# A two-branch conformer layer, forward and backward: four more normalised tiles and three copies out of PSUM on ScalarE instead of VectorE, in a new order of instructions

## The chip, the cores and the metric

The kernel runs on one core of one Trainium2 chip. The metric is the device time of one execution in microseconds (us). Five engines work side by side, each through its own queue of instructions in order: PE (TensorE, matmuls), DVE (VectorE), ACT (ScalarE), POOL (GpSimd) and SP (SyncE, here only the issuer of DMA transfers). They wait for each other through semaphores.

## The reference

A layer with two branches is computed for x of shape 2 x 4000 x 144 (bf16), and then its vector-Jacobian product for a given grad_out: the output and the gradients of x and of the seven weights. Cut to what matters:

```python
xa = _layernorm(x)                                   # (x - mean) / sqrt(var + eps)
q, k, v = split(xa @ w_qkv)
p = softmax(q @ k.T * D ** (-0.5))                   # 4000 x 4000 for each batch
glob = (p @ v) @ w_att_out
u, g = split(gelu(xa @ w_mlp_in))
loc = (u * dwconv(_layernorm(g), dw_csgu)) @ w_mlp_out
m = concat(glob, loc)
out = x + (m + dwconv(m, dw_merge)) @ w_merge        # 5 taps each
out, vjp = jax.vjp(layer, x, *weights); grads = vjp(grad_out)
```

## The kernel before

A batch's 4000 tokens are 32 tiles of 125 tokens (PB = 125); D = 144 is split into 128 and 16 rows wherever it is the contraction dimension. The attention of both batches is one loop over 64 tiles of queries. For each tile, `quad` (L1184) multiplies the queries with all keys, a chunk of 1000 keys at a time into a PSUM tile `ps`: 128 rows from `xaT_m` (L1187) and then the 16 remainder rows (L1194). `S_min` (L1209) moves the scores to `Pbuf` on DVE with a running minimum; after four chunks L1211 makes one number of the minima, and `P_exp` (L1215) does the Exp on ACT, in place. SP transposes the result by DMA to `PT` (L1219). Further on come dP (L1225 on ACT, L1226 on DVE, or L1223 on DVE alone) into `Sbuf`, its transposed form `ST` (L1405), the products `yz` with PT (L1236) and ST (L1266) and the gradient sums `X` (L1322, gathered in `acc` by L1327 and L1329). The work of the other branch and of the merge convolution is laid between the tiles; L590, L596, L621, L640 and L644 are its elementwise steps on DVE. The second batch is loaded and prepared while the first is still worked on: `gq` is its grad_out, `xa_aug` its x.

The head, up to the first Exp, concerns the first batch alone and works on four groups g of eight tiles. `ln_st` (L362) takes statistics on DVE, `ln_mv` (L368 to L373) makes the variance on DVE, and POOL raises it to the power −1/2 (L374); `ln_nm` (L378) makes minus mean over deviation, and `ln` normalises the eight tiles j of the group into `xa_aug`: on ACT where j is a multiple of four (L383, 8 tiles of 32), on DVE where it is odd (L385, 16), on POOL for the rest (L387, 8). Then `xat` transposes the group on PE: the main 128 rows into one PSUM tile, which ACT copies to `xaT_m` (L392, L393), and 112 rows into another, of which the last 16 are copied to `R` (L396, and L397 on DVE, 16 partitions x 1000 elements). From R, SP copies them to four partition groups `XR` (L399), out of which later tiles take the remainder rows; the first tile takes them out of R itself. `jit_q` and the following lines make a tile's queries (L1346 to L1349 `qb`, L1354 transposes, L1355 `qt`). At the same time the head fuses weights (L170 to L219: `two`, `Q`, `RW`, `cols`) and scales the merge weights tap by tap (`sWm`, L238 on ACT, L240 on POOL). `dwt` is the small DMA of the merge convolution's weights (L157), which PE needs at L215. 36 filler matmuls (`warm`, L192) lie between PE's first instructions.

No engine chooses what comes next. The class `Planner` holds a table `ORDER` with a list of numbers for each engine: the program's instructions (for PE, runs of them) are numbered as they are written, and the list says in which sequence they stand; each is chained to the one ahead of it on its engine. The lists have 1385 entries for PE, 2521 for DVE, 1642 for ACT, 423 for POOL and 826 for SP. They were written down as literal numbers, so every edit that adds or removes an instruction renumbers them.

Of the kernel before, what the change touches and what calls it, by code (L numbers as in the profile page):

```python
# [337 lines left out]
def pre_pieces(k, W, b, S, pst):  # L338
# [4 lines left out]
    if True:  # L343
# [36 lines left out]
        def ln(g):  # L380
            for j in range(8 * g, 8 * g + 8):
                if S.act_ln and j % 4 == 0:
                    nc.scalar.activation(S.xa_aug[:, j, 0:D], x_tp[:, j, :], ACT.Identity, scale=S.rstd_x[:, j:j + 1], bias=nmr[:, j:j + 1])  # L383
                elif j % 2:
                    nc.vector.tensor_scalar(S.xa_aug[:, j, 0:D], x_tp[:, j, :], S.rstd_x[:, j:j + 1], nmr[:, j:j + 1], op0=ALU.mult, op1=ALU.add)  # L385
                else:
                    nc.gpsimd.tensor_scalar(S.xa_aug[:, j, 0:D], x_tp[:, j, :], S.rstd_x[:, j:j + 1], nmr[:, j:j + 1], op0=ALU.mult, op1=ALU.add)  # L387

        def xat(g):
# [7 lines left out]
            nc.vector.tensor_copy(v8(S.R, 8 * g, 8)[96:112], pr[96:112, :, 0:PB])  # L397
# [378 lines left out]
class Planner:  # L776

    ORDER = {
# [1414 lines left out]
```

## Time and profile before

| | us |
|---|---|
| median of three runs | 1150.79 (1150.02 to 1152.15) |
| the profiled execution | 1152.39 |
| its span, from the first to the last instruction in the profile | 1150.5 |
| PE busy | 1118.8 |
| DVE busy | 1021.0 |
| ACT busy | 906.5 |
| POOL busy | 249.5 |

The profile is of one execution. A row of the timeline has its start (us from the span's beginning), its length, the engine, the line of the kernel, the operation, its output and input tiles with their sizes, how many instructions like it follow each other (xN, the length then is that of all of them), and in square brackets the idle time ahead of it with what ended that. PEld are PE's weight loads, and SPq and ACTq the issues of DMAs by these engines: their length is the issue's, not the transfer's. A row of the table by stage has the stage, its length, the busy time of PE, PEld, DVE, ACT and POOL (with the number of instructions), the granted clock of TensorE, the share of time in which the DMA engines were busy, and GB/s. A row of the waits says which engine at which line waited for what: us in total, how often, and the longest. Instructions of one engine overlap slightly, so the sum of their lengths can exceed the time between two starts.

### The profile page before, as it was taken

What the parts mean: (1) busy time and instruction counts of PE and PEld (TensorE: products, weight loads), DVE (VectorE), ACT (ScalarE), POOL (GpSimd) and SP (SyncE); (2) the same over time, 40 slices, a digit from 0 to 9 for tenths busy, and PEclk for the clock granted to TensorE, in tenths of its full rate; (3) what the DMA queues carried; (4) which work ended last, traced back from release to release, by engine and by line L of the source; (5) the groups of instructions that cost most, each with busy time, mean ns of one, the idle gap of its engine ahead of it and who ended that gap; (6) DMA issues with size and microseconds to landing.
All of it is one profiled execution on the core that took longest, in us unless ns stands there. A gap on an engine that the chain in (4) does not pass through costs nothing.

```text
span 1150.5 us, 35851 instructions
## 1 busy us (share of the span) xinstructions
PE 1118.8 (97%) x14293; PEld 868.7 (76%) x14293; DVE 1021.0 (89%) x3063; ACT 906.5 (79%) x1641; POOL 249.5 (22%) x427
## 2 busy tenths in 40 slices
PE   6999999999999999999999999999999999999998
PEld 3667777777777677777777777777777777699987
DVE  8699999999999998877999999999999997667656
ACT  5999898899898767777989889888889877615372
POOL 8111112111121113431001111111111112013642
PEclk9999999999999999999999999999999999999999
DMA  4688887979988989998988989888888899978973
GB/s 117 155 160 176 173 181 158 192 159 173 174 166 159 188 181 182 201 187 183 207 183 178 171 158 168 161 181 152 173 174 154 187 177 183 224 173 219 245 144 101
DMA packets 680887, 200.72 MB, mean 174 GB/s; under 512 B 657815, under 2 KB 674093, under 8 KB 680699
## 3 DMA queue, kind: packets, MB, share of 16 engines
q1 hardware_dynamic: 678352, 194.69, 84.6%
q0 software_dynamic: 2192, 3.62, 1.1%
q8 instruction: 111, 1.82, 0.7%
q14 instruction: 56, 0.46, 0.1%
q10 hardware_dynamic: 176, 0.12, 0.0%
HBM read 24.62 MB, written 18.01 MB: 37 GB/s over the span
## 4 chain that ended last, share of the span: by engine, by line
PE 64%; DMA 13%; DVE 11%; ACT 7%; issue 2%; SPq 1%; POOL 1%; ACTq 0%; DVEq 0%; POOLq 0%
PE X L1322 18%; PE ps L1187 14%; PE yz L1236 8%; PE yz L1266 8%; PE ps L1194 5%; DMA PT<-Pbuf 5%; DVE Pbuf L1209 4%; ACT Pbuf L1215 3%; PE po L1708 2%; DMA ST<-Sbuf 2%; PE pd L610 1%; DVE Sbuf L1226 1%; PE pj L1147 1%; ACT Sbuf L1225 1%; DMA go_h<-in_grad_out_dram 1%
## 5 line engine op out<-in xcount | busy, mean ns | idle before, releaser
L1209 DVE TENSOR_SCALAR_CACHE_REDUCE Pbuf<-ps 125x1000 bf16<-125x1000 f32 x256 | 306.2, 1197 | 30.1 <-PE ps L1194 22.4
L1225 ACT CAST Sbuf<-ps 125x1000 bf16<-125x1000 f32 x249 | 248.7, 999 | 86.7 <-PE ps L1194 66.2
L1215 ACT ACTIVATE Pbuf<-Pbuf,nm 125x1000 bf16<-125x1000 bf16 x256 | 284.9, 1144 | 4.4 <-DVE nm L1211 4.2
L1322 PE MATMUL X<-QBs,Pbuf 125*128 125x144 bf16 x2048 | 281.1, 226 | 0.2 <-POOL QBs L1256 0.2
L1322 PE MATMUL X<-QBs,Sbuf 125*128 125x144 bf16 x2048 | 281.3, 226 | 0.0
L1187 PE MATMUL ps<-xaT_m,qt 128*128 128x500 bf16 x1024 | 260.6, 374 | 5.0 <-DVE Pbuf L1209 3.5
L1322 PEld LDWEIGHTS <-Sbuf 125*128 125x128 bf16 x2048 | 198.2, 98 | 18.8 <-issue 18.5
L1322 PEld LDWEIGHTS <-Pbuf 125*128 125x128 bf16 x2048 | 200.2, 98 | 1.3 <-issue 1.1
L1226 DVE TENSOR_TENSOR Sbuf<-Sbuf,Pbuf 125x1024 bf16<-125x1024 bf16 x249 | 170.8, 690 | 7.9 <-ACT Sbuf L1225 6.0
L1236 PE MATMUL yz<-xa_aug,PT 125*128 125x145 bf16 x2048 | 151.0, 227 | 6.5 <-DMA PT<-Pbuf 6.4
L1266 PE MATMUL yz<-xa_aug,ST 125*128 125x144 bf16 x2048 | 150.8, 228 | 3.6 <-DMA ST<-Sbuf 2.4
L1236 PEld LDWEIGHTS <-PT 125*128 125x128 bf16 x2048 | 130.7, 98 | 21.6 <-DMA PT<-Pbuf 10.5
L1187 PEld LDWEIGHTS <-qt 128*128 128x128 bf16 x1024 | 91.4, 97 | 68.6 <-issue 7.0
L1266 PEld LDWEIGHTS <-ST 125*128 125x128 bf16 x2048 | 132.9, 98 | 12.2 <-issue 7.1
L1329 DVE TENSOR_TENSOR acc<-X,acc 125x432 f32<-125x432 f32 (+1 forms) x204 | 109.8, 548 | 15.3 <-PE X L1322 14.8
L1256 POOL TENSOR_TENSOR QBs<-g,g 125x144 bf16<-125x144 f32 x64 | 35.2, 550 | 379.2 <-ACT g L1255 290.9
L1194 PEld LDWEIGHTS <-qt 16*128 16x128 bf16 x1024 | 26.3, 91 | 108.9 <-issue 108.9
L1194 PE MATMUL ps<-XR,qt 16*128 16x500 bf16 x1016 | 100.4, 380 | 0.0
L681 POOL TENSOR_SCALAR l_w<-ring,nc,c 125x144 f32<-125x144 bf16 x64 | 31.8, 504 | 167.0 <-DVE nc L677 122.4
L653 DVE TENSOR_TENSOR l_prod<-ring,Wc 125x720 bf16<-125x720 bf16 x128 | 65.9, 535 | 0.2
L1611 PE MATMUL Hps<-Yg,go_h 125*128 125x144 bf16 x640 | 54.3, 226 | 0.0
L600 POOL TENSOR_TENSOR rsr<-ve,mhalf 125x2 f32<-125x2 f32 x32 | 25.4, 795 | 126.9 <-DVE ve L599 107.4
(540 smaller groups left out, 1946.4 us busy)
## 6 DMA issues: line engine op xcount, KB each, us to landing
Yn_d<-yn SPq DMA_DIRECT2D x64, 36.0 KB
Zn_d<-qb SPq DMA_DIRECT2D x64, 36.0 KB
ug_d<-ugr SPq DMA_DIRECT2D x32, 72.0 KB
Yg<-Yn_d SPq DMA_DIRECT2D x8, 288.0 KB
Yg<-ug_d SPq DMA_DIRECT2D x8, 288.0 KB
Zn<-Zn_d SPq DMA_DIRECT2D x4, 576.0 KB
PT<-Pbuf SPq DMA_TRANSPOSE x128
ST<-Sbuf SPq DMA_TRANSPOSE x128
```

Source lines behind the costliest of these rows:

```text
L653: nc.vector.tensor_tensor(prod[:, bi].rearrange("p a b -> p (a b)"), ring[:, a, p + bi:p + bi + 5, :].rearrange("p a b -> p (a b)"), W.Wc[ ...
L1187: mm = nc.tensor.matmul(pp[r // 2][:, r % 2, 0:CH], QT[i][:, 2 * h, :], bs(i)[0].xaT_m[:, c * CH:(c + 1) * CH], start=True, stop=False)
L1194: nc.tensor.matmul(pp[r // 2][:, r % 2, 0:CH], QT[i][rs, 2 * h + 1, :], xr, start=False, stop=True)
L1209: nc.vector.tensor_scalar(pv(pc(i, c2)), src, -1.0, 3.0e38, op0=ALU.mult, op1=ALU.min, accum_out=NM[i][:, c2:c2 + 1])
L1215: nc.scalar.activation(v, v, ACT.Exp, bias=NM[i][:, 4:5], scale=-1.0)
L1225: nc.scalar.copy(pv(sc(i, c2)), src)
L1226: nc.vector.tensor_tensor(sc(i, c2), sc(i, c2), pc(i, c2), op=ALU.mult)
L1236: nc.tensor.matmul(Yw, PT[0:PB, pos(i, j), :], S.xa_aug[:, j, 0:D + 1], start=(j == 0), stop=(j == NB - 1))
L1266: nc.tensor.matmul(Zw, ST[0:PB, j, :], S.xa_aug[:, j, 0:D], start=(j == 0), stop=(j == NB - 1))
L1322: nc.tensor.matmul(X[:, jj, :], l, r, start=(n_ == 0), stop=(n_ == len(ops) - 1))
L1329: nc.vector.tensor_tensor(av, X[0:PB, 0:nj, :], av, op=ALU.add)
L1611: nc.tensor.matmul(H[0:rows, a // 3, (a % 3) * D:(a % 3 + 1) * D], lhs, self.src[b][h][:, 2 + j, :], start=(n == 0 and a % 3 == 0), stop=( ...
```

## The change

Two lines of `pre_pieces` change. In `ln`, the tiles j = 3, 11, 19 and 27 of the first batch pass from DVE to ACT: ACT has 12, DVE 12, POOL 8 of the 32. In `xat`, the copy of the remainder rows to R passes from DVE to ACT for the groups 1, 2 and 3; group 0 keeps it on DVE.

```diff
-                if S.act_ln and j % 4 == 0:
+                if S.act_ln and j % 8 in (0, 3, 4):
...
-            nc.vector.tensor_copy(v8(S.R, 8 * g, 8)[96:112], pr[96:112, :, 0:PB])
+            (nc.scalar.copy if g else nc.vector.tensor_copy)(v8(S.R, 8 * g, 8)[96:112], pr[96:112, :, 0:PB])
...
     ORDER = {
-        "PE": [36, 37, 38, 39, 40, 41, 0, 1, 42, 2, 3, 4, 5, 43, 6, 7, 8, 44, 9, 10, 11, 53, 12, 45, 13, 46, 14, 47, 15, 16, 17, 48, 18, 54, 19, 49,
+        "PE": [36, 37, 38, 39, 40, 41, 0, 42, 1, 2, 3, 4, 43, 5, 6, 7, 44, 8, 9, 10, 53, 45, 11, 46, 12, 47, 13, 14, 15, 54, 16, 17, 18, 48, 19, 20,
```

All five lists of `ORDER` are replaced. DVE's now has 2514 entries and ACT's 1649, the others as many as before. On PE 542 of the 1385 runs stand at another place, by half a place on average and by ten at most; on POOL and SP single rows move by up to 54 and 68 places. The last 989 rows of PE, and what the other engines do beside them, are in the same order. In the head, dwt is now SP's fourth DMA (before its fourteenth), the 128-row part of w_qkv is issued on ACT ahead of the 16-row part, and PE multiplies chunk 1 of the first tile ahead of the transposes (L1354) of the next tile's queries. These are the places of which the prediction speaks.

ACT in the head, from its first weights to the first copy of transposed x. Before:

```order
L205 ACTIVATE RW<-hps 16x144
L205 ACTIVATE Q_283<-hps 128x144
L383 ACTIVATE xa_aug_114<-Sbuf,lnnm_101,rstd_x_65 125x144 x2
L217 CAST cols<-hps 128x2x5
L393 COPY xaT_m_118<-pt 128x1000
L238 ACTIVATE sWm_309<-raw,cols 128x144 x2
```

And of the change:

```order
L205 ACTIVATE Q_283<-hps 128x144
L217 CAST cols<-hps 128x2x5
L238 ACTIVATE sWm_309<-raw,cols 128x144
L205 ACTIVATE RW<-hps 16x144
L238 ACTIVATE sWm_309<-raw,cols 128x144
L218 CAST cols<-hps 16x2x5
L238 ACTIVATE sWm_309<-raw,cols 128x144
L219 ACTIVATE cols<-cols 128x4
L238 ACTIVATE sWm_309<-raw,cols 128x144
L383 ACTIVATE xa_aug_114<-Sbuf,lnnm_101,rstd_x_65 125x144 x3
L238 ACTIVATE sWm_309<-raw,cols 128x144 x2
L393 COPY xaT_m_118<-pt 128x1000
```

Four taps (sWm) and the casts for them have moved ahead of the normalised tiles of group 0, of which ACT now has three.

POOL in the head, from the power of group 2 to the tiles j18 and j22. Before:

```order
L374 TENSOR_TENSOR rstd_x_65<-lnve_100,mhalf 125x8
L2024 MEMSET A_dwc 128x240
L387 TENSOR_SCALAR xa_aug_114<-Sbuf,rstd_x_65,lnnm_101 125x144 x2
L374 TENSOR_TENSOR rstd_x_65<-lnve_100,mhalf 125x8
L65 MEMSET go_q_95 29x288
```

And of the change:

```order
L374 TENSOR_TENSOR rstd_x_65<-lnve_100,mhalf 125x8
L1119 MEMSET Pbuf 125x144x3
L240 TENSOR_SCALAR sWm_310<-raw,cols 128x144
L374 TENSOR_TENSOR rstd_x_65<-lnve_100,mhalf 125x8
L387 TENSOR_SCALAR xa_aug_114<-Sbuf,rstd_x_65,lnnm_101 125x144 x3
```

The two tiles of group 2 now stand behind the power of group 3, and a memset and a tap stand ahead of that.

SP while the second batch is loaded, from one store of Zn to the pair of PT transposes some 450 us into the kernel. Before:

```order
L1271 DMA Zn_d_71<-qb_128 128x144
L1405 DMA_TRANSPOSE ST<-Sbuf 128x16x128
L43 DMA xa_aug_8229<-in_x_dram 13x8x144
L1248 DMA Yn_d_69<-yn_132 128x144
L43 DMA gq<-in_grad_out_dram 13x576
L1405 DMA_TRANSPOSE ST<-Sbuf 128x16x128
L1219 DMA_TRANSPOSE PT<-Pbuf 128x16x128 x2
```

And of the change:

```order
L1405 DMA_TRANSPOSE ST<-Sbuf 128x16x128
L42 DMA gq<-in_grad_out_dram 112x576
L1271 DMA Zn_d_71<-qb_128 128x144
L42 DMA gq<-in_grad_out_dram 112x576 x2
L43 DMA gq<-in_grad_out_dram 13x576 x2
L1405 DMA_TRANSPOSE ST<-Sbuf 128x16x128
L43 DMA gq<-in_grad_out_dram 13x576
L1219 DMA_TRANSPOSE PT<-Pbuf 128x16x128 x2
```

Loads of gq and the store of Zn have moved between the first ST transpose and the PT pair. On DVE, some 74 us into the kernel, L621 stands two L1209 earlier than it did; before, it was two instructions ahead of the L1209 of which the prediction speaks.

More of the change, by code (lines that the diff above doesn't have):

```diff
@@ L778 @@
     ORDER = {
[51 rows of a table removed]
[51 rows of a table added]
             1347, 1342, 1348, 1337, 1343, 1324, 1353, 1344, 1345, 1349, 1346, 1352, 1325, 1350, 1361, 1363, 1362, 1365, 1364, 1354, 1355, 1369, 1371,
             1370, 1356, 1372, 1373, 1357, 1375, 1358, 1367, 1376, 1377, 1374, 1379, 1378, 1380, 1359, 1360, 1381, 1383, 1382, 1384, 1366, 1368],
-        "DVE": [0, 2, 1, 3, 4, 10, 5, 11, 9, 8, 6, 7, 12, 14, 15, 13, 16, 17, 40, 43, 25, 18, 44, 20, 22, 23, 19, 32, 24, 21, 34, 33, 35, 36, 26, 28,
[102 rows of a table removed]
-        "Activation": [1, 0, 4, 5, 2, 3, 7, 6, 8, 9, 10, 13, 29, 32, 14, 15, 11, 33, 16, 17, 18, 12, 37, 35, 34, 19, 20, 21, 24, 22, 23, 31, 27, 26,
[64 rows of a table removed]
-        "Pool": [8, 5, 15, 4, 11, 0, 12, 10, 1, 3, 47, 7, 2, 16, 18, 6, 19, 17, 41, 25, 26, 24, 50, 33, 32, 31, 9, 53, 37, 38, 20, 30, 42, 23, 13,
[43 rows of a table removed]
+        "DVE": [2, 1, 0, 3, 4, 5, 11, 10, 8, 6, 9, 7, 12, 14, 15, 16, 17, 13, 20, 25, 22, 23, 18, 24, 21, 19, 32, 41, 37, 28, 26, 33, 34, 35, 42, 29,
[102 rows of a table added]
+        "Activation": [0, 1, 2, 4, 3, 5, 6, 11, 36, 7, 40, 12, 45, 13, 42, 9, 8, 10, 39, 43, 14, 41, 15, 16, 19, 17, 18, 20, 37, 38, 21, 22, 23, 26,
[64 rows of a table added]
+        "Pool": [4, 10, 0, 50, 1, 6, 2, 7, 13, 8, 15, 9, 11, 16, 18, 19, 5, 17, 25, 26, 24, 41, 20, 31, 32, 33, 37, 47, 38, 14, 35, 22, 28, 30, 21,
[43 rows of a table added]
             805, 788, 813, 761, 821, 771, 789, 798, 804, 820, 797, 807, 822, 823, 814, 808, 806, 824, 825, 815],
```

518 rows, old and new, of the table ORDER are left out of this document.

## The prediction

> **What bounds the kernel now.** I read the page first (busy shares, slices), then a table by stage, then TensorE's waits, then the head instruction by instruction.
>
> ```profile
> PE 1118.8 (97%) x14293; PEld 868.7 (76%) x14293; DVE 1021.0 (89%) x3063; ACT 906.5 (79%) x1641; POOL 249.5 (22%) x427
> PE   6999999999999999999999999999999999999998
> ```
>
> TensorE is busy for 97% of the span, and its only poor slice is the first. The same by stage (columns: busy us of PE, PE's weight loads, DVE, ACT, POOL, then the granted clock):
>
> ```profile
> 0.00:28.60 28.60, 18.79 (x147) 11.43 (x147) 23.85 (x93) 15.60 (x45) 23.31 (x49) 1.00 0.45 117
> 28.60:100.00 71.40, 68.69 (x781) 49.31 (x780) 58.13 (x138) 68.08 (x138) 9.11 (x19) 1.00 0.76 164
> 520.00:1120.00 600.00, 591.11 (x7769) 471.14 (x7767) 522.47 (x1553) 461.58 (x817) 118.25 (x195) 1.00 0.90 182
> ```
>
> PE is idle for 9.8 us of the first 28.6 (28.60 − 18.79), for 2.7 of the next 71, and then for 1.5% (8.9 of 600). So the change, whose named edits all lie in the first 28 us, can only act there; behind it, a new order can only reshuffle the small waits. These are PE's three largest waits in the head, and then the largest of the rest of the kernel:
>
> ```profile
> PE hps L170 <- DMA raw<-in_w_qkv_dram: 6.3, 1, 6.3
> PE hps L215 <- DMA dwt<-in_dw_merge_dram: 1.4, 1, 1.4
> PE pt L1354 <- DVE R L397: 1.4, 1, 1.4
> ...
> PE yz L1236 <- DMA PT<-Pbuf: 6.4, 11, 1.0
> PE ps L1187 <- DVE Pbuf L1209: 3.5, 12, 0.9
> PE yz L1266 <- DMA ST<-Sbuf: 2.4, 3, 1.2
> ```
>
> Two head waits are named by the change's own parts: 1.4 us on the R copy of DVE, and 1.4 us on the DMA of dwt, which now is issued fourth instead of fourteenth. Much of PE's "busy" time in the head is filler, so what counts there is the chain to the first Exp; from then on PE is 96% busy (68.69 of 71.40), and what the first Exp gains or loses I pass on to the end one for one.
>
> **The change, part by part.** The chain's last links before, from PE, ACT and DVE:
>
> ```profile
> 21.78 0.60 PE L392 MATMUL pt<-ident,xa_aug 125*128 125x125 bf16 x8
> 23.36 0.72 ACT L238 ACTIVATE sWm<-raw,cols 128x144 bf16<-128x144 bf16 x2
> 23.98 0.98 ACT L393 COPY xaT_m<-pt 128x1000 bf16<-128x1000 bf16 x1
> 24.93 0.69 DVE L397 COPY R<-pt 16x1000 bf16<-16x1000 bf16 x1
> 26.50 0.59 PE L1194 MATMUL ps<-R,qt 16*128 16x500 bf16 x2
> 27.12 1.20 DVE L1209 TENSOR_SCALAR_CACHE_REDUCE Pbuf<-ps 125x1000 bf16<-125x1000 f32 x1 [0.19 <-PE ps L1194]
> 28.56 2.15 ACT L1215 ACTIVATE Pbuf<-Pbuf,nm 125x1000 bf16<-125x1000 bf16 x2
> ```
>
> *DVE loses* four tiles and three R copies. Four tiles take 1.00 us (row below), so 0.25 each and 1.0 in all; three copies at 0.69 are 2.07. Together 3.1 us less on an engine that was busy 16.34 of the 18.89 us of the stretch in which the chain runs:
>
> ```profile
> 21.26 1.00 DVE L385 TENSOR_SCALAR xa_aug<-Sbuf,rstd_x,lnnm 125x144 bf16<-125x144 bf16 x4
> 9.67:28.56 18.89, 16.60 (x135) 10.27 (x135) 16.34 (x63) 13.02 (x38) 15.82 (x31) 1.00 0.37 90
> 9.67 0.89 ACT L383 ACTIVATE xa_aug<-Sbuf,lnnm,rstd_x 125x144 bf16<-125x144 bf16 x2
> ```
>
> *ACT gains* them. A pair of its tiles takes 0.89, so four take 1.8. The trace has no 16x1000 copy on ACT. Bounds: 0.69 (DVE's row for the same copy) and 0.98 (ACT's copy of 128x1000, the same number of elements per partition). I take 0.98, the nearest row for engine and length: 2.9 for three. ACT gets 4.7 us into 18.89 − 13.02 = 5.9 us of idle time. It fits, but with 1.2 us to spare. [...]
>
> *What it does to the chain.* Let T be the time at which chunk 2's main transposes end, before 22.4 (21.78 + 0.60). ACT now runs four copies in a row from T: xaT of chunk 2, R, xaT of chunk 3, R. ACT's instructions overlap a little (the taps of 23.36 last 0.72, and the copy begins 0.62 behind them): 0.88 apart, the last R copy ends at T + 3 x 0.88 + 0.98 = T + 3.6; before, it ended on DVE at 25.62 = T + 3.2. Behind it now follow only the remainder matmuls, 0.59, and the 1.44 from L1209 to Exp (27.12 to 28.56): Exp at T + 5.7, against T + 6.2. So the new tail of the head is 0.45 **shorter** for equal T, although the copy itself is later.
>
> T is where the orders differ. Chunk 2's tiles j18 and j22 are POOL's:
>
> ```profile
> 13.31 0.69 DVE L397 COPY R<-pt 16x1000 bf16<-16x1000 bf16 x1 [1.20 <-PE pt L396]
> 15.59 0.30 DVE L373 TENSOR_SCALAR lnve<-lnve 125x8 f32<-125x8 f32 x1
> 13.37 0.74 POOL L1119 MEMSET Pbuf<- 125x432 bf16 x1
> 18.13 0.90 POOL L387 TENSOR_SCALAR xa_aug<-Sbuf,rstd_x,lnnm 125x144 bf16<-125x144 bf16 x2 [0.27 <-DVE lnnm L378]
> 19.00 1.64 POOL L374 TENSOR_TENSOR rstd_x<-lnve,mhalf 125x8 f32<-125x8 f32 x1
> ```
>
> POOL now does the power of group 2, the memset (0.74), a tap (0.37, near ACT's pair at 0.72), the power of group 3 (1.64) and only then j18 and j22 (0.9). Group 2's variance (L373) comes behind the first R copy on DVE, as before, with seven statistics instead of five ahead of it (about +0.6): 16.4 if that copy ends at 14.0 again. Then 16.4 + 1.64 + 0.74 + 0.37 + 1.64 + 0.9 = 21.7, the transposes of these last two tiles, T = 22.1: first Exp at 27.8, **0.75 early**. But the first R copy itself may move, for chunk 0's transposes do:
>
> ```profile
> 1.49 0.39 ACTq L154 DMA_DIRECT2D raw<-in_w_qkv_dram  x1
> 10.99 1.02 PE L392 MATMUL pt<-ident,xa_aug 125*128 125x125 bf16 x8
> ```
>
> In ACT's new order four taps and three small casts (4 x 0.36 plus, an estimate from the overlap, about 0.35: 1.8) stand between Q and its tiles, which began at 9.67 before. They now begin at 11.5, and three of them last till 12.8; the transposes, which ended at 12.0, end some 1.1 later. Against that, PE no longer waits for dwt, and the large part of w_qkv goes first on ACT's queue, one issue (0.4) earlier. I take +0.7 for the copy, which about cancels the 0.75. **Head: 0**, between −1.2 (the copy 0.4 early, nothing lost) and +0.7 (1.1 late, with some tenths of ACT's new load on the path).
>
> *The rest of the order.* One place gains plainly:
>
> ```profile
> 74.32 0.30 DVE L621 TENSOR_TENSOR ring<-dugr,hgr 125x288 bf16<-125x288 bf16 x1
> 74.54 0.45 DVE L644 TENSOR_TENSOR gpr<-l_sq,l_q 125x576 bf16<-125x576 bf16 x1
> 76.16 1.01 PE L1187 MATMUL ps<-xaT_m,qt 128*128 128x500 bf16 x4 [0.60 <-DVE Pbuf L1209]
> ```
>
> PE's 0.60 wait is for the L1209 that follows these two, and L621 (0.22 from start to start) has moved ahead of earlier work of DVE's, which in this stage is idle for 13 us (71.40 − 58.13): **−0.2**; 0, if it had no idle time just there. One place loses, SP between 452 and 463:
>
> ```profile
> 452.20 1.60 SPq L1405 DMA_TRANSPOSE ST<-Sbuf  x1
> 453.84 0.55 SPq L43 DMA_DIRECT2D xa_aug<-in_x_dram  x1
> 454.49 0.35 SPq L1248 DMA_DIRECT2D Yn_d<-yn  x1
> 454.89 0.69 SPq L43 DMA_DIRECT2D gq<-in_grad_out_dram  x1
> 455.76 3.12 SPq L1405 DMA_TRANSPOSE ST<-Sbuf  x1
> 458.98 3.78 SPq L1219 DMA_TRANSPOSE PT<-Pbuf  x2
> 463.52 0.56 PEld L1236 LDWEIGHTS <-PT 125*128 125x128 bf16 x9 [0.22 <-issue]
> ```
>
> From the first ST transpose to the PT pair three small transfers are issued, and PE takes up PT 0.8 us after the pair's issue. Now seven are, at about 0.45 each: PT is 1.8 later. PE's order moves the first L1236 only behind four more transposes (0.2 to 0.4). I take **+0.2**, since SP waits here for its data and part of the seven may fall into that; bounds 0 and +1.4. The other waits (some 16 us in the three rows above and smaller ones) I leave as they are, plus or minus 3: POOL's and SP's runs move by a handful of places everywhere with no one direction.
>
> *Sum.* 0 − 0.2 + 0.2 = 0 on the profiled execution's 1152.39 (span 1150.5 and 1.9 around it). That execution lies 1.6 above the median of the runs shown, 1150.79, so the forecast on the median is **1150.8**.
>
> **The rivals.**
> - *The head keeps what it was given.* If w_qkv lands early enough that ACT's taps are through before group 0's statistics, both PE waits of 1.4 fall away and nothing replaces them: −2.8, with −0.2 above 1147.8. For it: both waits are in the rows, and DVE's relief is real. Against: POOL's two powers before j18.
> - *SP becomes late where x and grad_out of the second batch are loaded.* The place is that of the last fence; it decides as soon as PT lands later than PE's 463.5, and there are no spare tenths. Each pair costs up to 1.4, and grad_out's second batch comes in loads like these all through this stretch, before tile after tile. Three pairs late is +4.2: 1155.0, **slower**. For it: four loads and a store pulled ahead in one place, and PT is PE's largest wait already. Against: PE reaches these transposes a little later too, and the loads have to be issued sometime.
> - *PE's slow start lasts longer.* Eight transposes took 1.02 at 10.99 and take 0.60 from chunk 1 on, with a granted clock of 1.00 in the stage's row:
>
> ```profile
> 17.82 0.60 PE L396 MATMUL pt<-ident,xa_aug 125*112 125x125 bf16 x8
> ```
>
>   With chunk 0 a microsecond later and fewer fillers ahead, chunk 1's sixteen transposes could still be slow: +0.9, 1151.7. [...]
>
> **How the numbers follow.** A measurement of this kernel can tell about 0.2%, 2.3 us, from no change. Head and order as summed (1150.8, its own range 1147 to 1153): 0.45. Full head gain (1147.8 and less where the small waits shrink too): 0.25. SP late: 0.25. PE slow: 0.05. The first splits 0.33 within, 0.06 faster and 0.06 slower; with the second faster, the third slower and the fourth within: faster 0.31, same 0.38, slower 0.31. The range runs from 1145.5 (the full head gain and 2 us of small waits) to 1156 (SP late at three places, the head +0.7).
>
> **What would show it.** Right: first Exp within 0.7 of 28.56, no PE wait for dwt or for R at L1354, ACT's 16x1000 copies at 0.95 to 1.0, chunk 0's transposes ending after 12.0, PE's wait for DVE at 76 us at 0.4. The gaining rival: first Exp below 27. The slower one: PE's waits for PT and ST between 437 and 520 us above 5 us. Wrong altogether: more than 3 us that lie behind 100 us and outside that stretch.

## The result and the profile after

The changed kernel takes 1156.98 us (median of 7 runs, 1155.99 to 1161.82) against 1150.79 for the kernel before on the same chip (7 runs, 1148.99 to 1152.72): ratio **1.0061**, 95% interval 1.0041 to 1.0081. By the ratio it is slower by 7.0 us, by the two medians by 6.2. The profiled execution of the changed kernel took 1155.99, with a span of 1154.2.

The page's busy shares and, below them, the table by stage of the changed kernel (busy us of PE, PE's weight loads, DVE, ACT, POOL; granted clock; DMA share; GB/s):

```profile
PE 1117.9 (97%) x14293; PEld 868.7 (75%) x14293; DVE 1012.7 (88%) x3056; ACT 910.6 (79%) x1648; POOL 249.9 (22%) x427
```

```profile
0.00:28.60 28.60, 18.45 (x143) 10.93 (x143) 21.14 (x86) 20.63 (x51) 21.49 (x47) 1.00 0.43 108
28.60:100.00 71.40, 69.71 (x789) 49.83 (x789) 58.38 (x142) 68.70 (x140) 11.79 (x22) 1.00 0.81 172
100.00:1030.00 930.00, 916.57 (x11603) 700.78 (x11602) 853.43 (x2474) 762.94 (x1332) 163.39 (x274) 1.00 0.87 176
1030.00:1154.20 124.20, 113.16 (x1765) 107.15 (x1762) 79.77 (x359) 58.32 (x128) 53.22 (x86) 1.00 0.69 171
```

The last two stages of the kernel before:

```profile
100.00:1030.00 930.00, 916.55 (x11567) 698.40 (x11565) 856.43 (x2471) 763.41 (x1332) 162.48 (x272) 1.00 0.90 177
1030.00:1150.50 120.50, 114.80 (x1807) 109.53 (x1804) 82.55 (x363) 59.45 (x129) 54.64 (x88) 0.99 0.75 178
```

Take PE's busy time from each stage's length. In the head PE is idle 10.2 us (9.8 before), in the next stage 1.7 (2.7), between 100 and 1030 us 13.4 (13.4), and behind 1030 us **11.0 (5.7)**. In these two profiles the whole difference lies in the last stage, where the second batch's merge convolution and the gradients of both batches are finished. None of the change's two edits is there; only the order is new. PE's waits, first the largest of the whole kernel:

```profile
PE yz L1236 <- DMA PT<-Pbuf: 5.5, 7, 1.2
PE hps L170 <- DMA raw<-in_w_qkv_dram: 4.5, 1, 4.5
PE pt L392 <- ACT xa_aug L383: 3.2, 1, 3.2
PE ps L1187 <- DVE Pbuf L1209: 2.7, 10, 0.4
...
PE yz L1266 <- DMA ST<-Sbuf: 1.7, 3, 0.7
```

and then those behind 1030 us alone, of the changed kernel and of the kernel before:

```profile
PE po L1708 <- DVE xo L1711: 2.4, 2, 2.0
PE po L1710 <- DMA VUsl<-VUs_d: 1.1, 1, 1.1
...
PE Hps L1611 <- DMA Yg<-Yn_d: 0.7, 1, 0.7
```

```profile
PE fpt L1826 <- ACT o L1854: 0.7, 1, 0.7
...
PE po L1708 <- DVE xo L1711: 0.4, 1, 0.4
```

The attention's waits, on PT, ST and L1209, are all a little smaller in this execution than before (6.4, 2.4 and 3.5); in a second profile of the changed kernel PT and ST have 6.8 and 3.2. The last stage has new ones. The largest is read from three engines' timelines of the changed kernel:

```profile
1062.69 1.29 POOL L1737 TENSOR_TENSOR dxo<-t,go_h 125x576 bf16<-125x576 f32 x1
1063.91 1.04 POOL L48 DMA_DIRECT2D out_dram<-dxo  x2
1070.82 1.27 POOL L1737 TENSOR_TENSOR dxo<-t,go_h 125x576 bf16<-125x576 f32 x1 [5.87 <-DMA out_dram<-dxo]
...
1065.35 0.91 DVE L1734 SCALAR_TENSOR_TENSOR t<-xa_aug,dx_s,acc 125x144 f32<-125x144 bf16 x3
1072.13 0.37 DVE L1734 SCALAR_TENSOR_TENSOR t<-xa_aug,dx_s,acc 125x144 f32<-125x144 bf16 x1 [5.87 <-POOL dxo L1737]
1073.38 0.45 DVE L1711 TENSOR_TENSOR xo<-po,xo 125x288 bf16<-125x288 f32 x1
...
1073.89 0.47 PE L1708 MATMUL po<-VUl,goT 128*125 128x144 bf16 x5 [1.95 <-DVE xo L1711]
```

It is a chain of three. `dxo`, POOL's sum for the gradient of x, has two buffers. Each sum is stored in two parts, 112 rows (L47) and 13 rows (L48). At 1063.91 POOL issues the L48 of two sums; the first belongs to the sum ahead of the one at 1062.69, and the next sum wants that buffer back: 5.87 us of waiting for POOL's own stores. DVE's next `t` (L1734) needs the buffer that this sum frees, and stands still for as long. L1711, which empties PE's PSUM tile `po`, is queued behind it, so PE runs out of tiles and waits 1.95. The kernel before has the same wait, with another queue behind it:

```profile
1077.56 1.28 POOL L1737 TENSOR_TENSOR dxo<-t,go_h 125x576 bf16<-125x576 f32 x1 [5.00 <-DMA out_dram<-dxo]
...
1076.51 0.46 DVE L1711 TENSOR_TENSOR xo<-po,xo 125x288 bf16<-125x288 f32 x1 [1.91 <-PE po L1710]
1078.87 0.65 DVE L1734 SCALAR_TENSOR_TENSOR t<-xa_aug,dx_s,acc 125x144 f32<-125x144 bf16 x2 [1.32 <-POOL dxo L1737]
...
1084.35 0.47 PE L1708 MATMUL po<-VUl,goT 128*125 128x144 bf16 x5 [0.37 <-DVE xo L1711]
```

There POOL sits idle for 5.00, but DVE still has an L1711 ahead of the blocked L1734 and loses 1.32; PE loses 0.37. (In a second profile of the kernel before, POOL's longest wait of this kind is 5.8 and PE's two waits for L1711 add up to 1.1.)

The head, its links in order of time in the changed kernel:

```profile
11.13 1.02 PE L392 MATMUL pt<-ident,xa_aug 125*128 125x125 bf16 x8 [3.24 <-ACT xa_aug L383]
13.25 0.69 DVE L397 COPY R<-pt 16x1000 bf16<-16x1000 bf16 x1 [0.83 <-PE pt L396]
...
21.14 0.93 PE L392 MATMUL pt<-ident,xa_aug 125*128 125x125 bf16 x8
22.15 0.52 ACT L383 ACTIVATE xa_aug<-Sbuf,lnnm,rstd_x 125x144 bf16<-125x144 bf16 x1
22.56 0.98 ACT L393 COPY xaT_m<-pt 128x1000 bf16<-128x1000 bf16 x1
23.57 0.98 ACT L397 COPY R<-pt 16x1000 bf16<-16x1000 bf16 x1
...
25.59 0.98 ACT L397 COPY R<-pt 16x1000 bf16<-16x1000 bf16 x1
...
28.74 1.13 ACT L1215 ACTIVATE Pbuf<-Pbuf,nm 125x1000 bf16<-125x1000 bf16 x1
```

The first Exp is at 28.74, 0.18 later than before: what was forecast for the head, though not by the way forecast (below).

### The profile page after: what moved, and what is told of

The parts are those of the page before. It is cut to its first block, busy times and chain, and to the rows that moved or that the text cites. A ratio compares the mean times of both kernels' runs of the same rounds, so it can differ in the third digit from the quotient of the medians.

```text
span 1154.2 us, 35863 instructions
## 1 busy us (share of the span) xinstructions
PE 1117.9 (97%) x14293; PEld 868.7 (75%) x14293; DVE 1012.7 (88%) x3056; ACT 910.6 (79%) x1648; POOL 249.9 (22%) x427
## 4 chain that ended last, share of the span: by engine, by line
PE 69%; DVE 9%; DMA 9%; ACT 6%; issue 3%; POOL 2%; SPq 1%; ACTq 0%; POOLq 0%; DVEq 0%
PE X L1322 20%; PE ps L1187 15%; PE yz L1266 9%; PE yz L1236 9%; PE ps L1194 5%; DVE Pbuf L1209 3%; DMA PT<-Pbuf 3%; PE po L1708 2%; DMA out_dram<-dxo 2%; PE pd L610 1%; PE pj L1147 1%; ACT Pbuf L1215 1%; DVE Sbuf L1226 1%; DMA ST<-Sbuf 1%; DMA goT<-ym 1%
## 5 line engine op out<-in xcount | busy, mean ns | idle before, releaser
L1209 DVE TENSOR_SCALAR_CACHE_REDUCE Pbuf<-ps 125x1000 bf16<-125x1000 f32 x256 | 305.9, 1195 | 32.7 <-PE ps L1194 25.1
L1322 PE MATMUL X<-QBs,Pbuf 125*128 125x144 bf16 x2048 | 281.5, 226 | 1.7 <-POOL QBs L1256 1.7
L1322 PE MATMUL X<-QBs,Sbuf 125*128 125x144 bf16 x2048 | 282.1, 226 | 0.1
L1187 PE MATMUL ps<-xaT_m,qt 128*128 128x500 bf16 x1024 | 260.5, 374 | 5.5 <-DVE Pbuf L1209 2.7
L1322 PEld LDWEIGHTS <-Sbuf 125*128 125x128 bf16 x2048 | 198.3, 98 | 19.1 <-issue 18.9
L1322 PEld LDWEIGHTS <-Pbuf 125*128 125x128 bf16 x2048 | 200.1, 98 | 1.5 <-issue 1.3
L1187 PEld LDWEIGHTS <-qt 128*128 128x128 bf16 x1024 | 91.6, 97 | 68.6 <-issue 5.6
L1735 ACT ACTIVATE t<-t,dx_c,rstd_x 125x144 f32<-125x144 f32 x64 | 29.2, 501 | 37.2 <-DVE t L1734 32.1
L1611 PE MATMUL Hps<-Yg,go_h 125*128 125x144 bf16 x640 | 54.3, 226 | 0.7 <-DMA Yg<-Yn_d 0.7
```

The source lines that it names most:

```text
L1187: mm = nc.tensor.matmul(pp[r // 2][:, r % 2, 0:CH], QT[i][:, 2 * h, :], bs(i)[0].xaT_m[:, c * CH:(c + 1) * CH], start=True, stop=False)
L1209: nc.vector.tensor_scalar(pv(pc(i, c2)), src, -1.0, 3.0e38, op0=ALU.mult, op1=ALU.min, accum_out=NM[i][:, c2:c2 + 1])
L1322: nc.tensor.matmul(X[:, jj, :], l, r, start=(n_ == 0), stop=(n_ == len(ops) - 1))
L1611: nc.tensor.matmul(H[0:rows, a // 3, (a % 3) * D:(a % 3 + 1) * D], lhs, self.src[b][h][:, 2 + j, :], start=(n == 0 and a % 3 == 0), stop=( ...
```

## The experiments

A single profile of this kernel says little about 2 us (runs of the kernel before reach from 1147.8 to 1157.4), so verdicts rest on ratios of timed runs, and on one quantity that is steady enough to be read from single traces: PE's time from the end of the last gradient matmul L1322 to the end of its last matmul. In every profile 1777 or 1778 matmuls fall into it. The rows that bound it, of the kernel before and of the changed one:

```profile
1031.54 0.29 PE L1322 MATMUL X<-M1T,qt 128*128 128x144 bf16 x2
...
1146.21 0.32 PE L1941 MATMUL fpt<-ident,dwmb 128*5 128x128 bf16 x2
```

```profile
1028.94 0.29 PE L1322 MATMUL X<-M1T,qt 128*128 128x144 bf16 x2
...
1149.99 0.32 PE L1941 MATMUL fpt<-ident,dwmb 128*5 128x128 bf16 x2
```

From 1031.83 to 1146.53 it is 114.7 in the first and from 1029.23 to 1150.31 it is 121.1 in the second. I call it **the last stretch**.

**1. Which part of the new order.** Hybrids take the order of one part from the changed kernel and the rest from the kernel before. e1 is the changed kernel with the old order of everything that began behind 1030 us, e2 the kernel before with the new order there. The edits of the lists, by the first numbers that differ in POOL's:

```diff
 e1, against the changed kernel
-        "Pool": [..., 374, 317, 323, 380, 321, 324, 376, 318, ...
+        "Pool": [..., 317, 323, 321, 324, 318, 319, 320, 325, ...
 e2, against the kernel before
-        "Pool": [..., 384, 327, 326, 328, 367, 330, 333, 332, ...
+        "Pool": [..., 327, 326, 328, 411, 380, 376, 374, 331, ...
```

> The changed kernel, with every instruction that began after 1030 us in the trace of before put back into the order of before on all five engines. Theory A (the time is lost in the tail's order): the changed kernel's trace is 2.6 us ahead of before when the attention ends and 3.8 behind at the end, so the tail's order costs 6.4; with the old tail this kernel takes 1150.8 - 2.6 = 1148 (1147 to 1150), and PE's waits behind 1027 us fall from 7 to about 2. Rival B (the added load on ScalarE or the head's order costs it): nothing in the tail matters, 1156 to 1157. Rival C (the lead in the attention is an accident of one execution): 1150.5 to 1152.

> The kernel before, with only the tail (what began after 1027 us in the changed kernel's trace) in the new order. Theory A: 1150.8 + 5.4 (the sum of PE's added waits in the tail) to + 6.4, so 1156 to 1157, with PE waiting about 2 us for the L1711 of DVE near 1075. Rival B: 1150.8. Rival C: in between.

Measured: e1 1155.48, ratio 1.0036 (1.0021 to 1.0050); e2 1154.50, ratio 1.0041 (1.0026 to 1.0056). The new order of the last part costs 4.7 us (0.41%, 0.26 to 0.56) on a kernel in which nothing else is changed: that is shown. Its middle is below theory A's 5.4 to 6.4, and the wait of 2 us for L1711 that I had expected in e2 is not there. The two largest of PE's waits behind 1030 us in e2 are others:

```profile
PE Hps L1611 <- DMA Yg<-Yn_d: 2.1, 1, 2.1
PE fpt L1826 <- ACT o L1853: 1.2, 1, 1.2
```

So the chain of three is what one profile of the changed kernel shows, and not the only way in which the new order loses time. Nor does e1 come back to the kernel before, as I had expected; something else in the changed kernel costs time too. Five of e1's twelve runs took 1151.08 to 1152.95 and seven 1155.07 to 1157.13. Both profiles of e1 (1152.95, and 1152.84 below) are of the lower kind, so no trace shows what the others lose.

**2. The new middle, and the head.** e5 is the kernel before with the new order between 50 and 1030 us. e6 has both edits and the new order up to 50 us, with the old order behind; e13 is the same kernel timed again. e3 has both edits, placed into the old order.

```diff
 e5, against the kernel before
-        "PE": [..., 110, 112, 113, 114, 118, 120, 121, 115, ...
+        "PE": [..., 112, 113, 110, 114, 118, 120, 121, 115, ...
 e6 and e13, against the changed kernel
-        "PE": [..., 112, 113, 110, 114, 118, 120, 121, 115, ...
+        "PE": [..., 110, 112, 113, 114, 118, 120, 121, 115, ...
 e3, against the changed kernel
-        "PE": [..., 42, 1, 2, 3, 4, 43, 5, 6, ...
+        "PE": [..., 1, 42, 2, 3, 4, 5, 43, 6, ...
```

> The kernel before, without the two edits: head (up to 50 us) and tail (from 1030 us) in the old order, all between in the new order. The first four runs split the loss: the new tail costs about 4 (old kernel with the new tail, and the difference between the changed kernel and the same with the old tail), and as much lies in the new head and attention together, though the profiled executions show no such loss there. Theory D (the attention's new order costs it): 1154 to 1155. Theory E (the head with its edits costs it, by a cause that the profiled executions did not have): 1150 to 1151.

> The changed kernel up to 50 us (both edits and the head's new order), and everything behind it in the order of before. Theory D: 1150 to 1151. Theory E: 1154 to 1155. In the profile the first Exp should lie within 0.5 us of 28.6 either way.

> The two edits alone: the four tiles and the three copies are on ScalarE, each placed behind the tile or copy of its group that ScalarE had already, and all else stands in the order of before. Theory A: the head gains at most 1 us or loses as much, 1150 to 1152. Rival B: 1154 or more, with the first Exp (28.56 before) later by 3 us.

> The kernel with both edits and the new head up to 50 us, the old order behind it, once more: its ratio was 1.0020 (1.0005 to 1.0036), while tiles alone and copies alone gave 0.9998 each. If both together cost something, the ratio is 1.0015 to 1.004 again; if the first measurement lay at the edge of its interval, 0.999 to 1.001. The first Exp is at 28.3 to 28.8 in both cases.

Measured: e5 1152.12, ratio 1.0005 (0.9990 to 1.0020): the middle costs nothing that can be told. e6 1154.29, 1.0020 (1.0005 to 1.0036), and e13 1153.50, 1.0015 (0.9997 to 1.0032): e6 lies just clear of 1 and e13's interval reaches it; together they put the head's price at about 2 us, with the first Exp at 28.49 and 28.66, hardly moved from 28.56. e3 1156.66, 1.0058 (1.0036 to 1.0080). In e3's head, the last R copy, the conversion of a weight queued behind it and the first Exp:

```profile
27.16 0.98 ACT L397 COPY R<-pt 16x1000 bf16<-16x1000 bf16 x1
28.17 0.28 ACT L172 COPY two<-hps 128x144 bf16<-128x144 bf16 x1
28.50 0.38 PE L181 MATMUL hps<-two,raw 128*128 128x144 bf16 x2 [1.22 <-ACT two L172]
...
31.41 2.15 ACT L1215 ACTIVATE Pbuf<-Pbuf,nm 125x1000 bf16<-125x1000 bf16 x2
```

Without a new order the two edits put the first Exp 2.85 us later: ACT's copies end 1.6 later than in the changed kernel, and PE waits for work of ACT's behind them. The new order of the head earns this back almost whole. The rest of e3's 0.58% is not placed; its granted clock comes up in the last section.

**3. Tiles or copies.** e8 is e6 with the three R copies back on DVE, e11 is e6 with the four tiles back on DVE. The lists of DVE and ACT change to match.

```diff
 e8, against e6
-            (nc.scalar.copy if g else nc.vector.tensor_copy)(v8(S.R, 8 * g, 8)[96:112], pr[96:112, :, 0:PB])
+            nc.vector.tensor_copy(v8(S.R, 8 * g, 8)[96:112], pr[96:112, :, 0:PB])
 e11, against e6
-                if S.act_ln and j % 8 in (0, 3, 4):
+                if S.act_ln and j % 4 == 0:
```

> The changed kernel's head with the four tiles on ScalarE, but the three copies to R on VectorE again, in the places at which VectorE is idle in the changed kernel (behind the tiles of groups 2 and 3 and the first L1209); old order behind 50 us. The same with the copies on ScalarE took 1.0020 of before. If the copies on ScalarE's queue cost the 2.3 us, this takes 1.000; if the rest of the head's new order does, 1.002. First Exp: chunk 3's copy comes 1 us earlier, so 27.5 to 28.0 against 28.5.

> The new head with the three R copies on ACT but the four tiles on DVE, and the old order behind 50 us: the counterpart of the kernel with the tiles alone. Theory C: the copies account for the head's 2.3 us (the tiles alone gave 0.9998): ratio 1.0015 to 1.004, 1152.5 to 1155, with the first Exp at 28.3 to 29. Rival D: the tiles and copies cost something only together, or the difference was within the noise: ratio 0.999 to 1.001.

Measured: e8 1150.64, ratio 0.9998 (0.9985 to 1.0011), first Exp 28.30 (27.5 to 28.0 was expected); e11 1151.78, 0.9998 (0.9986 to 1.0010), first Exp 28.53. After e8 I took the copies for the culprit; e11 refutes that. Neither edit costs anything that can be told by itself; only the two together seem to (e6 and e13).

Two more profiles, of e6 and of the kernel before once again, were taken to find the place.

```diff
 e6_again, against e6; before_again, against the kernel before
 (no line differs)
```

> The new head with the old order behind it, for another profile: the first was of a run at 1151.6, at the low end of 1150 to 1158. If a run near 1154 to 1158 is caught: its first Exp is late by the same amount if the head has two lengths; if the first Exp is at 28.5 again, the loss sits in waits further back.

> The kernel before, unchanged, for a second profile: its runs lie in two clusters, near 1148 to 1149.7 and near 1151 to 1153, and the first profile was of one at 1152.4. If this one is of the lower cluster, PE reaches the end of the attention about 2 to 3 us earlier than in the first (1031.8), and the waits that it lacks show what the two differ by.

They took 1153.78 and 1153.29. One row of PE's waits between 56 and 80 us in e6_again is new:

```profile
PE ps L1187 <- DMA qt<-qb: 2.3, 1, 2.3
```

SP ends its issue of the queries' DMA transpose at 59.87 us, and PE's L1187, which waits for it, starts at 62.95; e13 has 0.4 of this wait, e6 itself none, and e12 below, which shares e8's head and middle, has 2.1. So it comes and goes from one execution to the next, where new head and old middle meet. But e12's ratio is 1.0002, so it doesn't explain the 2 us of e6 and e13 either, and in no profile of the changed kernel's own order up to 1030 us (two of it whole, two of e1, and e4 and e9 below) is it seen. What the head costs there stays open.

**4. The chain of three in the last stage.** e4 attacks it at DVE: two L1711 stand ahead of the blocked L1734.

```diff
 e4, DVE against the changed kernel
 L1734 SCALAR_TENSOR_TENSOR t_19709<-xa_aug_8229,dx_s_19329,acc 125x144 x3
+L1711 TENSOR_TENSOR xo<-po,xo 125x288 x2
 L1734 SCALAR_TENSOR_TENSOR t_19778<-xa_aug_8229,dx_s_19329,acc 125x144
...
-L1711 TENSOR_TENSOR xo<-po,xo 125x288
...
-L1711 TENSOR_TENSOR xo<-po,xo 125x288
```

> The changed kernel with one place of VectorE's order altered: the two L1711 that stood behind the L1734 which waits 5.9 us for GpSimd (1072 us) stand ahead of it. Theory A, in its narrow form (that wait holds back the additions which free PE's PSUM tiles): PE's wait of 1.95 us at 1073.9 goes, and 1.5 to 2 us of the time with it: 1155.0 from 1157.0. If the wait only moves to the next addition or to a load of Yg, 1156.5 to 1157.

Measured: 1159.35, ratio 1.0083 (1.0064 to 1.0101): a miss. PE's wait did not go, it moved behind the next blocked L1734 (PE's timeline of e4):

```profile
1081.76 0.47 PE L1708 MATMUL po<-VUl,goT 128*125 128x144 bf16 x5 [0.58 <-DVE xo L1711]
...
1086.79 0.47 PE L1708 MATMUL po<-VUl,goT 128*125 128x144 bf16 x5 [1.37 <-DVE xo L1711]
```

I take it that POOL's wait was still there and took the next L1711 with it. e7 tried to single out an engine: e2's new order on PE, DVE, ACT and POOL, with SP in the old one.

```diff
 e7, against e2
-        "SP": [..., 720, 696, 690, 698, 691, 727, 723, 710, ...
+        "SP": [..., 696, 720, 721, 698, 699, 692, 689, 691, ...
```

> The kernel before with the new tail on PE, VectorE, ScalarE and GpSimd, and SP's transfers left in the old order. The new tail on all five engines cost 1.0041. If the late loads do it (Yg and VUsl, 2.4 us of PE's waits there), most of the loss goes: 1.000 to 1.002 of before. If the compute engines' order does it (GpSimd's L1737 waits 5.7 us for its own stores, VectorE and PE wait behind it; the sums for the weight gradients are late at L1826), the loss stays: 1.003 to 1.005.

Measured: 1164.83, ratio 1.0118 (1.0098 to 1.0138). One wait on L1711 alone now is 6.0 us (PE's waits behind 1030 us):

```profile
PE po L1708 <- DVE xo L1711: 6.0, 1, 6.0
```

A mixture is worse than either order, so e7 says nothing about which engine's order carries the loss, only that the five orders can't be mixed freely. Its last stretch is 129.5 us; PE is busy for 118.2 of it (113.0 in the kernel before), and the granted clock of the whole stage behind 1030 us is 0.94 (0.99 in the kernel before).

Two more profiles, of the changed kernel and of e1, were taken to see whether the last stage repeats.

```diff
 after_again, against the changed kernel; e1_again, against e1
 (no line differs)
```

> The changed kernel once more, for a second profile: its runs lie near 1156 and near 1160. The tail behind the last X matmul should be 124 to 125 us long again (118 to 121 with the old tail), and PE's waits there 5.5 to 7.

> The changed kernel with the old tail, once more: its runs lie near 1152 and near 1156, and the first profile was of one at 1153. If this one is near 1156, the waits that it has more show where the loss of the head and attention sits: in the attention by theory D, ahead of 50 us by theory E.

They took 1158.24 and 1152.84, with last stretches of 120.2 and 115.5. The length repeats. PE's waits in it repeat only in part: in the changed kernel's second profile the largest is for Yg (L1611, 2.0), and L1711 has 1.5, not 2.4.

**5. Taking POOL's wait away.** e9 is the changed kernel, e14 is e2, and e10 the kernel before, each with a third buffer for dxo. The room for it comes from one DVE junk buffer less and from c0 written over s1.

```diff
-        self.s1, self.s2, self.c0 = ([pm_.tile([PB, NB], F32, name="dx_%s%d" % (n, b)) for b in range(2)] for n in ("s1", "s2", "c0"))
+        self.s1, self.c0 = (2 * ([pm_.tile([PB, NB], F32, name="dx_s1%d" % b) for b in range(2)],)); self.s2 = [pm_.tile([PB, NB], F32, name="dx_s2%d" % b) for b in range(2)]
...
-            pj_ = wk.tile([PB, D], BF, tag="dxprod")
+            pj_ = wk.tile([PB, D], BF, tag="dxprod", bufs=1)
...
-        dxo = wk.tile([PB, GB, D], BF, tag="dxo")
+        dxo = wk.tile([PB, GB, D], BF, tag="dxo", bufs=3)
```

> The changed kernel whole, with a third buffer for POOL's sum dxo (room for it comes from one junk buffer less on DVE and from c0 written over s1). Theory A: the new order loses its 4 us behind 1030 us because POOL's L1737 waits 5 to 6 us for its own stores to leave the buffer and DVE, PE follow. Then the wait on out_dram<-dxo (13.7 us in four places) falls to a few us, TensorE's gaps in the last stage fall from 7.15 to below 3.5, the stretch behind the last L1322 from 125.0 to 120 to 121.5, and the time to about 1153 (ratio 1.0005 to 1.003). Rival B: POOL's wait is cover for something else (ACT's t at L1735, late loads of Yg and VUsl by SP), which then ends last: the wait goes, the gaps stay at 5.5 or more and the time at 1156 to 1158.

> The kernel before with the new order behind 1030 us alone (ratio 1.0041, 1.0026 to 1.0056, without a buffer more), now with the third buffer for dxo. Theory A (POOL's wait for its stores carries the new order's loss, all but about 1 us of loads of Yg and VUsl): ratio 1.000 to 1.002, the stretch behind the last L1322 from 124.5 to 119.5 to 121, TensorE's gaps in it from 5.62 to 2.5 to 4. Rival B (the loss lies in the order of TensorE and of SP's loads): ratio 1.003 to 1.005, the stretch 122.5 or more.

> The kernel before with the same third buffer, as a control. Its TensorE loses only 1.7 to 2.7 us in the last stage, so by theory A it gains 0 to 1.5 us: 1149.3 to 1150.8. By rival B 0: 1150.8. A gain of 3 us or more here would mean that the buffer is worth as much without the new order, and that e9 says nothing of the order.

Measured: e9 1156.13, ratio 1.0041 (1.0027 to 1.0055); e14 1152.72, 1.0012 (0.9995 to 1.0029); e10 1150.95, 0.9994 (0.9982 to 1.0006). What POOL's L1737 waited for behind 1030 us (us, times, longest), first in e2 and then in e14:

```profile
POOL dxo L1737 <- ACT t L1735: 26.0, 7, 9.4
...
POOL dxo L1737 <- DMA out_dram<-dxo: 15.1, 4, 5.6
```

```profile
POOL dxo L1737 <- ACT t L1735: 37.1, 10, 11.8
```

POOL's wait for its own stores (15.1 us in four places; 13.7 in four in the changed kernel, 8.4 in three before) is gone, and POOL waits for its data instead. (POOL's longest single wait in the new order, some 17 us for a load of grad_out or x ahead of its first sum, is there with the third buffer as without it.) The last stretch by kernel:

| kernels | last stretch, us | ratio to before |
|---|---|---|
| old order behind 1030 us (13 profiles) | 113.7 to 116.5, median 115.0 | 1 for the kernel before |
| new order there: the changed kernel twice | 121.1, 120.2 | 1.0061 |
| new order there: e2, e4 | 120.6, 119.8 | 1.0041, 1.0083 |
| new order and third buffer: e9, e14 | 117.1, 118.2 | 1.0041, 1.0012 |
| new order, SP's old: e7 | 129.5 | 1.0118 |

The buffer gives back 2.8 of the 5.4 us (mean 120.4 without it, 117.6 with it, 115.0 in the old order), and next to nothing in the kernel before. Of e2's 120.6, though, about 1.7 are not a wait: PE is busy for 115.0 of it and for 113.25 of e14's 118.2, and the granted clock of the stage is 0.98 in e2 and 1.00 in e14. PE's idle time in the stretch is 5.6 us in e2 and 4.95 in e14, against 7.15 and 6.65 in the changed kernel and 3.98 in e9. So the profiles of the changed kernel show the gain, those of e2 and e14 barely, and the timed ratios of e2 and e14 agree with it (1.0041 and 1.0012, with intervals that just overlap). Taken together they support that POOL's wait carries about half of the last stage's loss, and only in the new order. The waits that go with the buffer are not those for L1711 alone: those for L1826, behind small copies on ACT, fall from 1.6 to 2.0 us in the profiles without it to 0.2 and 0.3. PE's waits behind 1030 us in e14 name a candidate for the other half:

```profile
PE Hps L1611 <- DMA Yg<-Yn_d: 1.9, 1, 1.9
PE po L1710 <- DMA VUsl<-VUs_d: 0.9, 1, 0.9
```

They add up to 2.8 (in e9 1.7 and 0.8, 2.5), about the 2.6 that are left. SP's queue shows why VUsl is late: its last load, of the kernel before and then of the changed one:

```profile
1043.67 0.80 SPq L1635 DMA_DIRECT2D VUsl<-VUs_d  x2
```

```profile
1045.51 0.43 SPq L1635 DMA_DIRECT2D VUsl<-VUs_d  x1
```

Counted from the end of the last L1322 (1031.83 and 1029.23), the issue has moved from about 12.2 to 16.3 us, since loads of grad_out (`go_h`) and x now stand ahead of it. That these loads cost the other half is read from the waits and was not tried by itself.

Of the ratios, e14's agrees with theory A and e9's is above what it forecast (1.0005 to 1.003); PE's idle time fell less than forecast in both (to 4.95, not 2.5 to 4, and to 3.98, not below 3.5). As for e9: in the changed kernel the buffer returned 0.2% of 0.6%, with intervals that overlap. The rest there is put down to the other half of the last stage and the part that e1 still has (1.0036).

**6. A better kernel.** e12 is e8 with the third buffer, the parts that had cost nothing.

```diff
 e12, against e8: the lines of experiment 5
-        dxo = wk.tile([PB, GB, D], BF, tag="dxo")
+        dxo = wk.tile([PB, GB, D], BF, tag="dxo", bufs=3)
```

> The new head with the four tiles alone on ACT, the old order behind 50 us, and the third buffer for dxo: the candidate for a kernel faster than both. By theory A 1149 to 1150.5 (ratio 0.9985 to 0.9995), since the old order's last stage has at most 1 to 3 us of gaps to give; by rival B 1150.6 as without the buffer.

Measured: 1151.69, ratio 1.0002 (0.9986 to 1.0018). No kernel of this study beats the kernel before by more than its interval; the nearest is e10 (0.9994).

## Why the prediction was wrong

Forecast was 1150.8, no change; it became slower by 6 us and lies above the upper end of the range.

- **First Exp at 28.56, between −1.2 and +0.7: right, but by luck, through two terms that failed and cancelled.** T, the end of chunk 2's transposes, came at 22.07 (21.14 and 0.93), where 22.1 was worked out without the late copy. From there the first Exp was to follow at T + 5.7. The last ACT copy was to end at T + 3.6 and ended at T + 4.5: ACT had a tile of group 3 in hand (22.15, 0.52) and took up the copies 0.49 late, and they started 1.01 apart, not 0.88, three times: 0.39 more. Against that the 0.7 that I had added for a later first R copy did not come: it started at 13.25, not after 13.31. The size of the new operation was right: 0.98.
- **PE's waits for dwt and for R at L1354: gone, as forecast.** The gaining rival failed because a new wait took their place: 3.24 for ACT's tiles at chunk 0's transposes. Those transposes ended at 12.15, only 0.15 later than before and not 1.1: ACT's three tiles were forecast from 11.5 to 12.8 and ran from 10.19 to 11.48. That is why the 0.7 for the first R copy did not come.
- **The wait for L1209 at 76 us:** the longest wait for L1209 is now 0.4, as forecast. It is worth 0.2.
- **SP between 437 and 520 us: the forecast that named the right sign for the wrong reason.** The rival that ends slower was put there, with 1155.0; PE's waits for PT and ST there are 0.7 us (1.2 before), far from the 5 that would have shown it. Over the whole kernel they differ no more than two executions of one kernel do (7.2 and 10.0 changed, 8.8 and 7.5 before), and e5, which contains that stretch, costs nothing that can be told. PE's slow start did not last either: chunk 1's main transposes take 0.61 at 16.96, chunk 0's 1.02 at 11.13 (1.02 at 10.99 before); why the first are slower, no run shows.
- **The step that failed: "The other waits … I leave as they are, plus or minus 3: POOL's and SP's runs move by a handful of places everywhere with no one direction."** The change moves single rows of POOL and SP by up to 54 and 68 places, and behind 1030 us the moves cost more than the 3 allowed for the whole kernel: e2 has nothing but this part of the change and costs 0.41% (0.26 to 0.56), 4.7 us. That is also the sign named for "wrong altogether": PE's idle time behind 1030 us grew by 5.3. In that stage PE depends on DVE for each PSUM tile `po`, DVE on POOL for each buffer `t`, and POOL on the landing of its own stores; in the kernel before DVE's work stands so that a 5 us stall of POOL costs PE 0.4 (1.1 in the second profile). The row that said so was in the trace of before (the 5.00 at 1077.56), and I read no timeline there, because PE's waits in it were small. A small wait beside a long idle time of the engine behind it can be cover, and a new order can lose it.
- **"What the first Exp gains or loses I pass on to the end one for one": not settled.** e6 and e13 cost about 2 us with a first Exp that has hardly moved, so the first Exp does not seem to be the whole price of a head. Where these 2 us sit, and the rest of e1's 0.36% beside them, is not known. Only the hybrids' own wait for qt was found, and the changed kernel does not have it. From the first Exp to the last L1322 the profiles take 1000.0 to 1004.8 us whatever their order (1000.5 and 1003.6 for the changed kernel, 1003.3 and 1000.6 for the kernel before), so 2 us can't be found there by single profiles.

So of the 7 us, 4 to 5 are placed behind 1030 us, and that is shown. About half of them is put down to POOL's wait for its stores, on the evidence of the third buffer; the other half is put down to later loads by the waits alone. What lies ahead of 1030 us, 2.3 us by the difference and 4.1 by e1, stays open.

## What to carry to other kernels

When a change brings a new order for the whole program, ask stage by stage how much waiting time of the slower engines is hidden today, not only how long the bounding engine waits: a queue in which PE waits 0.4 us beside an engine that stands still for 5 may be held together by its order alone. Here the stores from a ring of two buffers made POOL, which issues them, wait 5.87 us ahead of a later sum, and DVE, which feeds the ring, stood still for as long. Another buffer removed POOL's wait (15.1 us in e2, none in e14), and another order (e4) moved PE's. To find the place of a loss, put parts of the new order into the old kernel before theorising about any of them.

## What was not expected of the hardware

- **POOL's stores land late.** From issue to landing the two L48 stores of dxo between 1060 and 1072 us took 6.7 us (the transfers' median, 14.6 KB each in the list of DMA issues):

```profile
out_dram<-dxo POOLq DMA_DIRECT2D x2, 14.6 KB, 6.7
```

  It varies: in the kernel before, three small ones between 1060 and 1080 us took 3.9, and two of 126.0 KB 7.6.

- **The clock in the head is not the same in every execution.** In a second profile of the kernel before, the head's granted clock was 0.94, not 1.00, and its first Exp stood at 30.28, not 28.56; e14, with the same head, had 0.94 too. The head's row in that second profile:

```profile
0.00:28.60 28.60, 18.54 (x136) 12.18 (x136) 22.41 (x90) 14.91 (x40) 23.15 (x49) 0.94 0.45 116
```

  That is 1.7 us from one execution to the next with no change in the program, about what e6 and e13 cost in all: a single profile can't show such a cost.

- **Behind the head, too, the granted clock differs between executions.** By stage (up to 28.6, 100 and 1030 us, and behind) it reads 0.99 or 1.00 throughout in thirteen of the twenty profiles. The other seven are the two above, e6_again (0.98 from 28.6 to 100 us), e4 (0.98 there and in the head), e3 (0.95 there and 0.98 behind 1030 us), e2 (0.98 behind 1030 us) and e7 (0.94 there). In e6_again the row from 60 to 100 us is

```profile
60.00:100.00 40.00, 36.43 (x414) 26.88 (x412) 34.84 (x96) 35.41 (x69) 5.56 (x9) 0.96 0.79 161
```

  where e6 has 1.00. Counted as that share of the 40 us, an estimate, it is 1.6 us of full clock. PE has a long wait in some of these stages: 2.3 us in e6_again, 2.1 in e2, 6.0 and 2.5 in e7. But waits as long stand in stages at 1.00 (2.1 in e12, 1.95 in the changed kernel), so no rule follows from these traces.

  This is a candidate for the open part that no experiment here tried. The mean granted clock of the timed runs is 0.9983 in e6 (0.9994 in the runs of the kernel before beside them), 0.9986 in e13 (0.9988), 0.9982 in e1 (0.9993) and 0.9960 in e3 (0.9993). Counted as that share of 1150 us, an estimate, the differences are worth 1.3, 0.2, 1.3 and 3.8 us.
